# Attention, a Fourier mix and a feed-forward layer on one core: two blocks of the first layer share a PSUM bank

## The chip, the cores and the metric

The kernel runs on one core of a Trainium2 chip. The metric is device time in microseconds (us): the median over several executions. Before the change it is 1330.21 us, from 3 runs between 1328.94 and 1335.06.

A core has five engines that work at the same time, each through a queue of its own in order: TensorE (PE; its weight loads are listed as PEld), VectorE (DVE), ScalarE (ACT), GpSimd (POOL) and SyncE (SP, which here only issues transfers). PE writes its results into PSUM, a memory of eight banks, each with 512 fp32 values per partition. ACT and DVE read them from there.

## What is computed

```python
def reference(q, k, v, w_ch1, w_ch2):      # q, k, v: (8, 8, 576, 64)
    x = block_causal_attention(q, k, v)    # softmax, blocks of 64; laid out (8, 576, 512)
    X = fft(fft(x, axis=1), axis=2)
    u = x + real(X)
    un = (u - mean(u)) / sqrt(var(u) + 1e-6)          # over the last axis
    return u + maximum(un @ w_ch1, 0) @ w_ch2         # 512 -> 2048 -> 512
```

## The kernel before

**Three kinds of work.** For each of 64 heads: maxima of the scores (`max_part`, line 371), scores and exponentials (`scores`, line 417) and the product with V (`values`, line 441). For each of 8 batches: the Fourier mix (`fourier_steps`, line 522), by matmuls with cosine and sine tables. And the feed-forward: the 4,608 rows are cut into 18 feeds of 256 rows (`feed_steps`, line 725), each of which starts when its rows are normalized and turned (`normalized_steps`, line 678).

**Precision.** Products are made from fp16 parts: a value is split into a high and a low part, and three matmuls (high x high, low x high, high x low) stand for one. So an intermediate has to leave PSUM twice: as its rounded high part, and as the difference to it.

**A feed.** The hidden layer of 2,048 is cut into 16 blocks of 128. The first layer of block f is the function `first` (line 729): four parts of three matmuls, each with 256 moving columns, into one half (256 of 512 columns) of a bank of the pool `h`, which has two banks. Behind the fourth part ACT writes `gh`, the relu in fp16 (line 743), and DVE writes `gl`, what is left of it (line 744). `gh` and `gl` have three buffers each. The second layer of block f is `second` (line 746): for each half of the rows three matmuls of 512 columns (with `gh` twice and with `gl` once) are added into one of two banks `acc`. After block 15 DVE adds the result to `u` (line 755), and SP stores it. All matmuls are issued by a helper, so that their line is 194 (line 197 for transposes). In the profile the tiles tell them apart: `h<-uh,W` and `h<-ul,W` for the first layer, `acc<-W,gh` and `acc<-W,gl` for the second.

**The order inside a feed** (lines 776 to 780): the first layer of block 0, then always the first layer of block f+1 and the second layer of block f.

**The planner.** The order in which instructions are issued is made at build time, by a loop at line 909. Work comes in steps (`Step`, line 137): a cost on PE in us, a chain of costs on other engines (A for ACT, D for DVE, G for POOL, Q for SP's queue), the keys that must be done before, and the key that it sets. The planner keeps a clock `now` for PE and a list of booked times for each other engine. It picks, among the steps of attention and the transform that are ready, the one with the earliest place. Where none is ready it takes the next step of the feeds, the filler, if that is ready. The lines that matter here:

```python
yield Step(
    lambda part=part: first(f, part), 0.327, ("A0.4", "D0.44") if last else (), after,
    ("g", me, f) if last else None,
)
```

Here 0.327 is the cost of three matmuls on PE, and A0.4 and D0.44 are what ACT and DVE are booked for at the end of a block. The key `("g", me, f)` says when block f has left PSUM: `second_steps(f)` waits for it, and `first_steps(f + 2)`, which takes the same bank. The queues of ACT and DVE follow the order in which the steps are issued, whichever kind of work they belong to.

Up to the first feed the three matmul pools (`ps`, `h`, `acc`) are lent to attention as well (`lent`, line 252). From then on attention and the transform have the three banks `ps` alone. The first feed (`me == 1`) also waits for its weights (`"w"`).

Of the kernel before, what the change touches and what calls it, by code (L numbers as in the profile page):

```python
# [9 lines left out]
F32 = mybir.dt.float32  # L10
F32R = mybir.dt.float32r
F16 = mybir.dt.float16
# [10 lines left out]
P = 128  # L23
NF = FF // P
NK = DM // P
# [153 lines left out]
def tile_attn_fourier_ffn(  # L179
# [5 lines left out]
    work = pool("work")  # L185
    ps_av = pool("ps_av", 1, space=PSUM)
    ps = {name: pool(name, n, space=PSUM) for name, n in BANKS.items()}
# [5 lines left out]
    def mm(*args, **kw):  # L193
        return tc.keep_in_program_order(nc.tensor.matmul(*args, **kw))  # L194
# [43 lines left out]
    for at in range(0, NCOS, P):  # L238
        w = min(P, NCOS - at)
        nc.vector.tensor_scalar(ZT[:, at:at + w], ones[0:34, 0:w], 0.0, None, op0=ALU.mult)  # L240

    W = const.tile([P, 2 * NF + 2, 2, DM], F16, name="W")
# [14 lines left out]
    def ready(step):  # L257
        r = max((done[x] for x in step.after), default=0.0)
        return max(r, min(rings[x][0] for x in lent)) if step.bank else r
# [418 lines left out]
    def normalized_steps(us, keys, stores, place):  # L678
# [17 lines left out]
        def turn(i):  # L696
            un = uns.pop(i)
            if i == 0:
                parts.extend(work.tile([P, NK, 2, P], F16, name=x, bufs=2) for x in ("uh", "ul"))
            uh, ul = parts  # L700
            t = ps_tile()
            for c in range(NK):
                tp(t[:, P * c:P * (c + 1)], un[:, P * c:P * (c + 1)], ident)
            tv = t.rearrange("p (c n) -> p c n", c=NK)
            nc.scalar.copy(uh[:, :, i], tv)
            nc.vector.tensor_tensor(ul[:, :, i], tv, uh[:, :, i], op=ALU.subtract)
            if i == 1:
                feeds.append(feed_steps(me, uh, ul, us, stores))
# [16 lines left out]
    def feed_steps(me, uh, ul, us, stores):  # L725
        acc = []
        gs = {}

        def first(f, part):
            fs = slice(P * (f % NK), P * (f % NK + 1))  # L730
            if part == 0:
                gs[f] = ps["h"].tile([P, 512], F32, name="h")[:, 0:2 * P]
            t = gs[f]
            i = 3 * part
            for w, x_ in ((0, uh), (0, ul), (1, uh)):
                mm(t, W[:, NK * (f // NK) + part, w, fs], x_[:, part], start=(i == 0), stop=(i == 3 * NK - 1))
                i += 1
            if part < NK - 1:
                return
            gh = work.tile([P, 2 * P], F16, name="gh", bufs=3)  # L740
            gl = work.tile([P, 2 * P], F16, name="gl", bufs=3)
            gs[f] = gh, gl
            nc.scalar.activation(gh, t, AF.Relu)  # L743
            nc.vector.scalar_tensor_tensor(gl, t, 0.0, gh, op0=ALU.max, op1=ALU.subtract)  # L744

        def second(f, n):
            if f == 0:
                acc.append(ps["acc"].tile([P, DM], F32, name="acc"))
            gh, gl = gs[f]
            ns = slice(P * n, P * (n + 1))  # L750
            for j, (g_, w) in enumerate(((gh, 0), (gh, 1), (gl, 0))):
                mm(acc[n], g_[:, ns], W[:, NF + f, w], start=(f == 0 and j == 0), stop=(f == NF - 1 and j == 2))
            if f == NF - 1:
                u = us[n]
                nc.vector.scalar_tensor_tensor(u, acc[n], inv_w, u, op0=ALU.mult, op1=ALU.add)
                stores[n](u)

        def first_steps(f):
            for part in range(NK):
                last = part == NK - 1  # L760
                after = (("t", me, 0), ("t", me, 1)) + ((("g", me, f - 2),) if f > 1 else ()) if part == 0 else ()
                if me == 1:
                    after += (("w", NK * (f // NK) + part),)
                yield Step(
                    lambda part=part: first(f, part), 0.327, ("A0.4", "D0.44") if last else (), after,
                    ("g", me, f) if last else None,
                )

        def second_steps(f):
            for n in range(2):  # L770
                yield Step(
                    lambda n=n: second(f, n), 0.648, ("D0.76",) if f == NF - 1 else (), (("g", me, f),) + ((("w", NF + f),) if me == 1 else ()),
                    ("F", me) if f == NF - 1 and n == 1 else None,
                )

        yield from first_steps(0)
        for f in range(NF):
            if f + 1 < NF:
                yield from first_steps(f + 1)
            yield from second_steps(f)  # L780


    stage = [utile() for _ in range(3)]
# [125 lines left out]
    while True:  # L909
# [22 lines left out]
        if soon:  # L932
            i = min(soon, key=lambda i: heads[i].place)
        elif feed and ready(filler) <= now or feed and not able:
            i = None
        elif able:
            i = min(able, key=lambda i: ready(heads[i]))
# [60 lines left out]
```

## Time and profile before

| | |
|---|---|
| median of 3 runs | 1330.21 us |
| profiled execution, its own time | 1334.54 us |
| its span, first to last instruction | 1332.8 us |
| PE busy | 1193.2 us, 90% |
| DVE, ACT, POOL busy | 53%, 43%, 40% |
| mean granted clock of PE | 0.963 of full speed |
| matmuls of the feeds, first to last | from 186 us to the end |

An engine is busy while one of its instructions runs. A wait is the idle time before an instruction, and it is put down to whatever released that instruction last. A duration in a timeline reaches from an instruction's start to its acknowledged end; the next instruction of the engine can start before that. Idle time of an engine that is not the bottleneck costs nothing by itself.

### The profile page before, as it was taken

The page shows a single profiled execution, that of the slowest core. Times are in us where ns is not written, and L with a number is a line of the kernel's source. Part 1 is how long each engine was busy: PE and PEld are TensorE (multiplying, and loading weights), DVE is VectorE, ACT ScalarE, POOL GpSimd, SP SyncE. Part 2 cuts the span into 40 slices and gives each one's busy share as a digit, 9 for nine tenths or more (in the row PEclk, how much of TensorE's full clock was granted, in tenths as well). Part 3 has the DMA queues.
Part 4 walks back from the last instruction along what each step waited for, and adds up shares of the span by engine and source line. Part 5 has one row for each costly group of instructions (what it writes and reads, how often), then busy time and mean ns, then how long its engine had stood idle before and what let it go on. Part 6 is the DMA issues. An engine that isn't in the chain of part 4 may idle for free.

```text
span 1332.8 us, 25628 instructions
## 1 busy us (share of the span) xinstructions
PE 1193.2 (90%) x10068; PEld 892.8 (67%) x10068; DVE 702.9 (53%) x1584; ACT 567.2 (43%) x1281; POOL 533.1 (40%) x578
## 2 busy tenths in 40 slices
PE   2565379999999998999999998999999999999998
PEld 2455257767776776767777676777767667666665
DVE  6984687565646757564555654457433433312221
ACT  3569357544545555445545444454322212111111
POOL 4479244546544853654544474344600302100000
PEclk9997679989899999999999898999999999999999
DMA  9655313332332233234333223230011000000000
GB/s 281 218 154 176 108 32 83 99 91 60 82 103 76 61 85 105 59 80 108 94 80 96 65 60 90 75 96 25 21 32 34 23 17 21 17 1 17 16 17 16
DMA packets 55943, 99.10 MB, mean 74 GB/s; under 512 B 7709, under 2 KB 26605, under 8 KB 55696
## 3 DMA queue, kind: packets, MB, share of 16 engines
q1 hardware_dynamic: 52176, 87.56, 23.4%
q0 software_dynamic: 2288, 7.54, 1.9%
q10 hardware_dynamic: 1360, 2.38, 0.6%
q8 instruction: 79, 1.29, 0.4%
q14 instruction: 40, 0.33, 0.1%
HBM read 58.46 MB, written 18.87 MB: 58 GB/s over the span
## 4 chain that ended last, share of the span: by engine, by line
PE 71%; DVE 9%; POOL 4%; ACT 3%; issue 2%; DMA 2%; DVEq 0%; SPq 0%; POOLq 0%; ACTq 0%
PE h L194 25%; PE acc L194 25%; PE ps L194 14%; PE av L194 5%; POOL pl L436 2%; DVE tmp L549 2%; PE ps L197 1%; DVE M L392 1%; DMA U<-xd,rows 1%; DVE rest L308 1%; DVE tmp L550 1%; DVE fs L518 1%; DVE W L856 1%; DVE gl L744 1%; ACT lead L293 1%
## 5 line engine op out<-in xcount | busy, mean ns | idle before, releaser
L194 PE MATMUL h<-uh,W 128*128 128x256 f16 x2304 | 455.3, 276 | 0.0
L436 POOL TENSOR_TENSOR pl<-p,ph 128x288 f16<-128x288 f32 (+1 forms) x256 | 256.8, 1013 | 355.6 <-ACT p L435 229.6
L194 PEld LDWEIGHTS <-W 128*128 128x128 f16 x3456 | 325.4, 99 | 89.9 <-issue 5.4
L194 PE MATMUL acc<-W,gh 128*128 128x512 f16 x1152 | 348.6, 385 | 0.0
L194 PE MATMUL h<-ul,W 128*128 128x256 f16 x1152 | 316.7, 275 | 0.0
L744 DVE SCALAR_TENSOR_TENSOR gl<-h,gh 128x256 f16<-128x256 f32 x288 | 120.8, 420 | 294.2 <-ACT gh L743 292.5
L743 ACT ACTIVATE gh<-h 128x256 f16<-128x256 f32 x288 | 110.2, 383 | 369.1 <-PE h L194 358.6
L194 PE MATMUL acc<-W,gl 128*128 128x512 f16 x576 | 220.8, 383 | 5.3 <-DVE gl L744 5.2
L194 PE MATMUL ps<-lead 72*128 72x64 f32 (+9 forms) x696 | 198.4, 344 | 9.7 <-ACT lead L293 6.7
L434 ACT ACTIVATE ph<-ps 128x288 f16<-128x288 f32 (+1 forms) x236 | 119.7, 508 | 94.2 <-PE ps L194 92.8
L194 PE MATMUL av<-VH,pl 128*128 128x65 f16 x960 | 118.6, 202 | 38.8 <-POOL pl L436 36.9
L194 PEld LDWEIGHTS <-gh 128*128 128x128 f16 x1152 | 101.8, 99 | 65.6 <-issue 6.8
L392 DVE TENSOR_REDUCE M<-ps 128x1 f32<-128x320 f32 (+3 forms) x227 | 117.3, 531 | 43.1 <-PE ps L194 41.9
L194 PEld LDWEIGHTS <-ph 128*128 128x128 f16 x1920 | 114.6, 104 | 36.4 <-issue 12.3
L194 PEld LDWEIGHTS ps<-lead 73*128 73x128 f32 (+1 forms) x696 | 125.7, 200 | 19.0 <-ACT lead L293 6.7
L194 PE MATMUL av<-VH,ph 128*128 128x65 f16 x960 | 120.8, 203 | 14.7 <-DVE x L474 11.8
L194 PE MATMUL ps<-rest 128*128 128x64 f32 (+2 forms) x357 | 126.3, 360 | 4.0 <-DVE M L392 3.3
L310 POOL TENSOR_TENSOR rest<-raw,lead 64x576 fp32r<-64x576 f32 x64 | 117.8, 1840 | 24.7 <-ACT lead L293 19.3
L435 ACT ACTIVATE p<-ps 128x288 f32<-128x288 f32 (+1 forms) x236 | 119.5, 507 | 13.0 <-POOL pl L436 10.2
L194 PEld LDWEIGHTS <-pl 128*128 128x128 f16 x960 | 94.7, 103 | 42.4 <-POOL pl L436 40.3
L194 PE MATMUL av<-VL,ph 128*128 128x64 f16 x960 | 120.0, 201 | 0.0
L194 PEld LDWEIGHTS <-gl 128*128 128x128 f16 x576 | 56.8, 99 | 77.8 <-DVE gl L744 9.5
(171 smaller groups left out, 1393.7 us busy)
## 6 DMA issues: line engine op xcount, KB each, us to landing
raw<-in_qk_dram SPq DMA_DIRECT2D x64, 288.0 KB
rest<-lead SPq DMA_DIRECT2D x112, 144.0 KB
W<-in_moe_w_ch_dram SPq DMA_DIRECT2D x14, 1024.0 KB
V<-in_v_dram SPq DMA_DIRECT2D x32, 320.0 KB
xd<-x SPq DMA_DIRECT2D x32, 256.0 KB
out_dram<-u SPq DMA_DIRECT2D x32, 256.0 KB
u<-xd SPq DMA_DIRECT2D x8, 512.0 KB
dft<-in_c_dft_dram POOLq DMA_DIRECT2D x1, 2606.0 KB
```

The source lines that it names most:

```text
L194: return tc.keep_in_program_order(nc.tensor.matmul(*args, **kw))
L197: return tc.keep_in_program_order(nc.tensor.transpose(*args, **kw))
L293: nc.scalar.copy(LEAD[h % NB][0:D, 64:], raws[h])
L308: nc.vector.tensor_tensor(x0[0:D, 0:S], raw[:, 0:S], x1[0:D, 64:64 + S], op=ALU.subtract)
L310: nc.gpsimd.tensor_tensor(x0[D:P, S:], raw[:, S:], x1[0:D, 64 + S:], op=ALU.subtract)
L392: nc.vector.tensor_reduce(m[:, j:j + 1], t[:, at - hi:at], axis=AX.X, op=ALU.max)
L434: nc.scalar.activation(ph[:, at:at + w], t[:, 0:w], AF.Exp, scale=0.125)
L435: nc.scalar.activation(p32[:, 0:w], t[:, 0:w], AF.Exp, scale=0.125)
L436: nc.gpsimd.tensor_tensor(pl[:, at:at + w], p32[:, 0:w], ph[:, at:at + w], op=ALU.subtract)
L549: nc.vector.tensor_tensor(e[0:r], X[c][0:r], U[c][0:r], op=op)
L743: nc.scalar.activation(gh, t, AF.Relu)
L744: nc.vector.scalar_tensor_tensor(gl, t, 0.0, gh, op0=ALU.max, op1=ALU.subtract)
```

## The change

Blocks are handled in pairs. The even block takes the left half of a bank of `h`, the odd block the right half. Only the first matmul of the even block clears the bank (`start`), and only the last of the odd block closes it (`stop`). Then one ACT instruction and one DVE instruction, of 512 columns each, take both blocks out; `gh` and `gl` are twice as wide and have two buffers each in place of three. The order inside a feed goes by pairs: the first layers of blocks 0 and 1, then always the first layers of the next pair and the second layers of the pair before. The planner's steps follow: the chain (now A0.6, D0.72) hangs on the last part of the odd block, the key `("g", me, f)` stands for a pair, and the first layer of an even block waits for the pair two before. The number of matmuls and their shapes stay.

```diff
@@ feed_steps
         def first(f, part):
             fs = slice(P * (f % NK), P * (f % NK + 1))
-            if part == 0:
-                gs[f] = ps["h"].tile([P, 512], F32, name="h")[:, 0:2 * P]
-            t = gs[f]
+            if f % 2 == 0 and part == 0:
+                gs[f] = ps["h"].tile([P, 512], F32, name="h")
+            t = gs[f - f % 2]
+            half = t[:, 2 * P * (f % 2):2 * P * (f % 2 + 1)]
             i = 3 * part
             for w, x_ in ((0, uh), (0, ul), (1, uh)):
-                mm(t, W[:, NK * (f // NK) + part, w, fs], x_[:, part], start=(i == 0), stop=(i == 3 * NK - 1))
+                mm(
+                    half, W[:, NK * (f // NK) + part, w, fs], x_[:, part], start=(f % 2 == 0 and i == 0),
+                    stop=(f % 2 == 1 and i == 3 * NK - 1), skip_group_check=True,
+                )
                 i += 1
-            if part < NK - 1:
+            if f % 2 == 0 or part < NK - 1:
                 return
-            gh = work.tile([P, 2 * P], F16, name="gh", bufs=3)
-            gl = work.tile([P, 2 * P], F16, name="gl", bufs=3)
-            gs[f] = gh, gl
+            gh = work.tile([P, 4 * P], F16, name="gh", bufs=2)
+            gl = work.tile([P, 4 * P], F16, name="gl", bufs=2)
+            for x in range(2):
+                gs[f - 1 + x] = (gh[:, 2 * P * x:2 * P * (x + 1)], gl[:, 2 * P * x:2 * P * (x + 1)])
             nc.scalar.activation(gh, t, AF.Relu)
             nc.vector.scalar_tensor_tensor(gl, t, 0.0, gh, op0=ALU.max, op1=ALU.subtract)
...
         def first_steps(f):
             for part in range(NK):
-                last = part == NK - 1
-                after = (("t", me, 0), ("t", me, 1)) + ((("g", me, f - 2),) if f > 1 else ()) if part == 0 else ()
+                last = f % 2 == 1 and part == NK - 1
+                after = ()
+                if part == 0 and f % 2 == 0:
+                    after = (("t", me, 0), ("t", me, 1)) + ((("g", me, f - 4),) if f > 3 else ())
                 if me == 1:
                     after += (("w", NK * (f // NK) + part),)
                 yield Step(
-                    lambda part=part: first(f, part), 0.327, ("A0.4", "D0.44") if last else (), after,
-                    ("g", me, f) if last else None,
+                    lambda part=part: first(f, part), 0.327, ("A0.6", "D0.72") if last else (), after,
+                    ("g", me, f - 1) if last else None,
                 )
...
-                    lambda n=n: second(f, n), 0.648, ("D0.76",) if f == NF - 1 else (), (("g", me, f),) + ((("w", NF + f),) if me == 1 else ()),
+                    lambda n=n: second(f, n), 0.648, ("D0.76",) if f == NF - 1 else (),
+                    (("g", me, f - f % 2),) + ((("w", NF + f),) if me == 1 else ()),
...
         yield from first_steps(0)
-        for f in range(NF):
-            if f + 1 < NF:
-                yield from first_steps(f + 1)
-            yield from second_steps(f)
+        yield from first_steps(1)
+        for f in range(0, NF, 2):
+            for steps in (first_steps, second_steps):
+                for x in range(2):
+                    if steps is second_steps:
+                        yield from steps(f + x)
+                    elif f + 2 < NF:
+                        yield from steps(f + 2 + x)
```

## Rows read from the trace of the kernel before

**Rows 1.** The page, part 1: busy time, share of the span, instructions

```profile
PE 1193.2 (90%) x10068; PEld 892.8 (67%) x10068; DVE 702.9 (53%) x1584; ACT 567.2 (43%) x1281; POOL 533.1 (40%) x578
```

**Rows 2.** Busy time by stage: window, its length, busy (instructions) per engine, clock, DMA

```profile
0.00:186.00 186.00, 91.20 (x688) 77.48 (x689) 137.75 (x257) 99.92 (x200) 103.29 (x103) 0.86 0.55 172
186.00:966.00 780.00, 741.95 (x6882) 567.31 (x6883) 454.35 (x1082) 399.41 (x909) 396.08 (x420) 0.97 0.29 77
966.00:1332.80 366.80, 360.08 (x2501) 248.03 (x2499) 110.79 (x247) 67.90 (x173) 33.77 (x55) 1.00 0.06 19
```

**Rows 3.** Waits of PE in 186 to 966: total, times, longest

```profile
PE av L194 <- POOL pl L436: 12.9, 11, 4.2
PE ps L194 <- DVE M L392: 7.2, 7, 2.7
...
PE acc L194 <- DVE gl L744: 3.1, 3, 1.7
```

**Rows 4.** Waits of PE from 966 to the end

```profile
PE acc L194 <- DVE gl L744: 2.1, 2, 1.8
```

**Rows 5.** Timeline 1151 to 1154, a steady stretch: start, length, instruction, [idle before]

```profile
1151.14 0.38 ACT L743 ACTIVATE gh<-h 128x256 f16<-128x256 f32 x1 [2.22 <-PE h L194]
...
1151.56 0.42 DVE L744 SCALAR_TENSOR_TENSOR gl<-h,gh 128x256 f16<-128x256 f32 x1 [2.18 <-ACT gh L743]
...
1153.54 0.59 PE L194 MATMUL acc<-W,gh 128*128 128x512 f16 x2
```

**Rows 6.** Timeline 971 to 977, the longest late eviction

```profile
971.80 0.38 ACT L743 ACTIVATE gh<-h 128x256 f16<-128x256 f32 x1 [2.22 <-PE h L194]
...
976.14 0.42 DVE L744 SCALAR_TENSOR_TENSOR gl<-h,gh 128x256 f16<-128x256 f32 x1
...
976.62 0.39 PE L194 MATMUL acc<-W,gl 128*128 128x512 f16 x1 [1.82 <-DVE gl L744]
```

**Rows 7.** Timeline, PE's three other waits for gl, and waits soon after

```profile
214.91 0.39 PE L194 MATMUL acc<-W,gl 128*128 128x512 f16 x1 [0.67 <-DVE gl L744]
...
742.50 0.39 PE L194 MATMUL acc<-W,gl 128*128 128x512 f16 x1 [1.71 <-DVE gl L744]
...
745.22 0.24 PE L194 MATMUL av<-VH,ph 128*128 128x65 f16 x1 [1.15 <-DVE M L394]
...
907.12 0.39 PE L194 MATMUL acc<-W,gl 128*128 128x512 f16 x1 [0.74 <-DVE gl L744]
...
910.45 1.09 PE L194 MATMUL ps<-dft,fs 128*128 128x290 f32 x3 [1.27 <-DVE fs L518]
```

**Rows 8.** Groups of 186 to 966, shapes apart: busy us, mean ns, idle before

```profile
L744 DVE SCALAR_TENSOR_TENSOR gl<-h,gh 128x256 f16<-128x256 f32 x160 | 66.7, 417 | 73.3 <-ACT gh L743 71.5 <-issue 1.2
L434 ACT ACTIVATE ph<-ps 128x512 f16<-128x512 f32 x110 | 66.0, 600 | 33.2 <-PE ps L194 32.1
...
L743 ACT ACTIVATE gh<-h 128x256 f16<-128x256 f32 x160 | 61.1, 382 | 126.3 <-PE h L194 115.8 <-DVE vacc L333 5.0 <-PE ps L194 3.4
...
L706 DVE TENSOR_TENSOR ul<-ps,uh 128x512 f16<-128x512 f32 x20 | 13.4, 679 | 1.4 <-ACT uh L705 1.4
```

**Rows 9.** Timeline of ACT, three in a row without a wait

```profile
806.58 0.59 ACT L435 ACTIVATE p<-ps 128x512 f32<-128x512 f32 x1
807.06 0.39 ACT L743 ACTIVATE gh<-h 128x256 f16<-128x256 f32 x1
807.32 0.62 ACT L434 ACTIVATE ph<-ps 128x512 f16<-128x512 f32 x1
```

**Rows 10.** Windows at the lower clock, behind late evictions

```profile
742.90:749.70 6.80, 5.65 (x35) 4.48 (x34) 2.79 (x9) 0.40 (x1) 0.00 (x0) 0.50 0.00 1
...
910.10:913.50 3.40, 3.05 (x10) 2.26 (x11) 3.34 (x10) 1.33 (x3) 0.00 (x0) 0.50 0.00 0
```

**Rows 11.** Two of eight equal windows of 186 to 966

```profile
478.50:576.00 97.50, 92.74 (x870) 70.54 (x869) 60.43 (x147) 48.81 (x112) 50.98 (x57) 1.00 0.33 85
...
771.00:868.50 97.50, 91.80 (x809) 68.74 (x810) 47.22 (x120) 44.82 (x101) 51.09 (x60) 0.95 0.27 73
```

## The prediction

> **What bounds the kernel now.** I read the page's list of engines first: TensorE (PE) is busy for 90% of the span, and no other engine is above 53% [rows 1]. That share is an average over three stages, so the second view is the busy time by stage [rows 2]. Up to 186 us PE has no feed-forward work yet and is idle for 94.8 us; the diff leaves this stage alone, since no block of the first layer runs in it. From 186 to 966 attention, the transform and the feed-forward share the engines; PE is busy for 741.95 of 780 us, so it is idle for 38.05. From 966 on, only the rest of the transform and the feed-forward are left, and PE is idle for 366.8 - 360.08 = 6.7 us, most of it behind its last matmul, where the result leaves. PE is the bound, and the feed-forward is what fills it wherever attention leaves room: whatever is not done by 966 is done after it. So the time moves by two things only: PE's own work, and PE's idle time or slower clock.
>
> The third view is who PE waits for. In the middle stage its largest waits are for POOL's `pl` (12.9 us) and for DVE's maxima (7.2 us), both in the attention heads; the feed-forward's own wait, for `gl`, is 3.1 us in three pieces [rows 3]. In the last stage the waits for `gl` are PE's only ones: 2.1 us in two pieces [rows 4]. These 5.2 us are all that PE loses directly to the eviction that the change rewrites. The timeline of a steady stretch shows why it is so little: a block's relu starts at 1151.14, `gl` is finished at 1151.56 + 0.42 = 1151.98, and the second layer first reads that block at 1153.54 [rows 5]. There are 1.56 us to spare, since the second layer of the block before and the first layer of the block behind stand between.
>
> **The change, part by part.**
>
> *PE's work.* The 12 matmuls of a block and the 6 of its second layer stay, with the same shapes and weights; only their order and two flags differ. Cost nothing: the engine that bounds issues the same list.
>
> *The evictions.* Out go 2 ACT instructions of 0.382 us and 2 DVE instructions of 0.417 us for each pair of blocks; in come one of each over 512 columns. The trace has no relu of that width, but it has ACT reading 128x512 from PSUM into f16 in 0.600 us and DVE subtracting into 128x512 f16 in 0.679 us [rows 8]; I take these. By durations a pair saves 2 x 0.382 - 0.600 = 0.164 us on ACT and 2 x 0.417 - 0.679 = 0.155 on DVE; over the 80 pairs of the middle stage (160 blocks, [rows 8]) that is 13 and 12 us. But durations overlap when instructions stand in a row: there the 512-wide one holds ACT for 807.06 - 806.58 = 0.48 us and the relu of 256 columns for 807.32 - 807.06 = 0.26 [rows 9], so a pair frees only 2 x 0.26 - 0.48 = 0.04 us, 3 us in the stage. The freed share is 1 to 3% of what ACT (399.41 us) and DVE (454.35 us) do there [rows 2]. PE's waits there other than for `gl` are 38.05 - 3.1 = 35 us; if they shrink by as much, that is 0.3 to 1.1 us. Bounds: nothing, and 13 us if every microsecond freed on ACT were one that PE waits for. I take **-0.5**, near the low end, because the largest of these waits is for POOL, which gets nothing.
>
> *The order.* Before, a block's second layer follows its last first-layer matmul by one second-layer and one first-layer block, about 2.4 us from the relu's start [rows 5]; afterwards by two of each, about twice that. The pair's eviction takes 0.600 + 0.679 = 1.28 us, so 1.56 us to spare become 2 x 2.4 - 1.28 = 3.5, or 2 more. At the head of a feed one block stands between before, two afterwards. In the last stage DVE finished one `gl` at 976.56, although its relu began at 971.80, because DVE's queue had transform work ahead of it; PE lost 1.82 us [rows 6]. The 2 us more to spare cover that, and the other 0.3 us of that stage [rows 4]. Nothing follows there that would wait for DVE instead, since all that PE still does is feed-forward: **-2.1**.
>
> In the middle stage it is otherwise. Two of the three waits fell while DVE was far behind, and PE met DVE again soon after: 1.15 us at 745.22, behind the wait at 742.50, and 1.27 us at 910.45, behind the one at 907.12 [rows 7]. PE takes its instructions in order; arriving earlier, it would wait there for as much longer. Of 3.1 us only the 0.67 at 214.91 has no wait for DVE close behind it: **-0.7**, with ends 0 and -3.1.
>
> *Buffers.* The two banks and two pairs of `gh`/`gl` hold as many blocks as the order needs: pair k takes the bank of pair k-2, and its `gh` buffer, after all of pair k-1's first layer and pair k-2's second have been issued. Cost nothing in steady order; the cover is that distance, and if it is gone the price is the eviction of 1.28 us itself. No DMA is added, and no queue of SP or POOL is passed.
>
> *The planner.* The order of PE is written by a planner with new costs and due times, so from the first feed on attention's steps fall elsewhere among the blocks, and the 35 us of other waits and the slower stretches are dealt anew. I count this as nothing on average. For its size I use how the eight equal windows of the stage differ. In the one that loses least PE is idle for 97.5 - 92.74 = 4.8 us at full clock; in the one that loses most it is idle for 5.7, and a clock of 0.95 takes another 4.9 [rows 11], together 10.6. So a window deals some 2 us either way of the middle of these, and eight of them, if independent, 2 x the root of 8, about 6 us: an estimate.
>
> **Sum:** -0.5 - 2.1 - 0.7 = -3.3 us. The rows are of an execution that took 1334.54 us (a span of 1332.8 and 1.7 around it), 4.3 above the median of 1330.21; I take the difference from the median: **1327 us**, and 0.25% is not to be told from nothing (a measurement of this kernel tells about 0.5%, 6.65 us, from no change).
>
> **The rivals.**
>
> *A, faster: the waits for `gl` also cost clock.* Behind the wait at 742.50 the granted clock is 0.50 (the 1.2 GHz level) for 6.8 us, and behind that at 907.12 for 3.4 us [rows 10], with PE busy almost throughout, so half of each is lost. If the late evictions go and nothing takes their place, the gain is 5.2 + 3.4 + 1.7 + 0.5 = 10.8: 1319.4 us. For it: in both stretches PE had just been idle. Against it: the waits behind them [rows 7] would leave PE idle as well.
>
> *B, slower: the longer instruction stands in front of a head.* A pair's relu holds ACT 0.218 us longer than a block's, and its `gl` DVE 0.262 longer, in one piece. Where they come just ahead of the exponentials that `pl` is made from, or of a maximum, PE's 11 + 7 waits for these [rows 3] each grow by 0.48: 8.6 us, 1338.8 us. It decides from 14 of those 18 (6.65 / 0.48) on. For it: both queues are in order. Against it: there are half as many such pieces, and POOL, not ACT, is the late one in 11 of the 18.
>
> *C, much slower: the banks no longer rotate.* The first block of a pair now waits in its bank until the second is done, and its eviction no longer lies beside the second's matmuls; if PE had to stand by, all 144 pairs would pay 1.28 us, 184 us: 1514 us. Against it: two banks are left, and 4.8 us between a pair and its reader. The Trainium skill, Perfetto Trace Analysis, "Optimizing Tensor Performance", asks that independent groups of matmuls rotate through different PSUM banks so that one's evacuation overlaps the next one's matmuls; inside a pair the change does the opposite. The trace bears it out so far as [rows 5] have the eviction beside the next block's matmuls; but that block's partner can stand there as well as the next pair.
>
> **How the numbers follow.** The forecast (no measurable change) has a chance of 0.51, A 0.33, B 0.14, C 0.02. So faster by over 0.5% is 0.33, within it 0.51, slower 0.16. The range starts below A, at 1314, where A meets a part of the 13 us bound on the freed time, and ends at 1337, between the planner's 6 us and a little more over the forecast and B. The forecast's own range is 1319 to 1335.
>
> **What would show it.** ACT's and DVE's groups on `h` should have 144 instructions each, near 0.60 and 0.68 us. PE's matmuls should be as many and as long. PE's waits for `gl` should be under 1 us in all, and PE after 966 idle only at the end. Waits for `pl` and the maxima should stay near 20 us. The prediction is wrong if PE's idle time between 186 and 966 falls or rises by more than 6 us, if the lower clock shows clearly less or more often, or if the 512-wide evictions take much more than the rows say.

## The result: 1317 us, and the profile after

The changed kernel takes 1317.41 us (median of 9 runs, 1312.82 to 1322.97) against 1330.44 for the kernel before (9 runs, 1326.45 to 1335.06). The ratio is 0.9904, 95% interval 0.9887 to 0.9921: about 13 us faster, and clear of the 0.5% bound. That is inside the range given (1314 to 1337), on the side that had a chance of 0.33, and just below the forecast's own range (1319 to 1335).

The profiled execution took 1312.82 us, the fastest of the nine; its span is 21.9 us shorter than that of [rows 1], while the medians differ by 13.0. The two profiles therefore show in sum more gain than there is.

The groups of the two evictions, with the columns of [rows 8], but over the whole span (from the page):

```profile
L750 DVE SCALAR_TENSOR_TENSOR gl<-h,gh 128x512 f16<-128x512 f32 x144 | 98.8, 686 | 232.4 <-ACT gh L749 232.0
...
L749 ACT ACTIVATE gh<-h 128x512 f16<-128x512 f32 x144 | 85.9, 597 | 292.4 <-PE h L194 292.2
```

Half as many (144 pairs in 288 blocks), at 0.597 and 0.686 us; 0.600 and 0.679 were assumed.

A steady stretch of the last stage, to be read against [rows 5]:

```profile
1154.07 0.60 ACT L749 ACTIVATE gh<-h 128x512 f16<-128x512 f32 x1 [4.61 <-PE h L194]
...
1154.70 0.69 DVE L750 SCALAR_TENSOR_TENSOR gl<-h,gh 128x512 f16<-128x512 f32 x1 [4.52 <-ACT gh L749]
...
1159.08 0.59 PE L194 MATMUL acc<-W,gh 128*128 128x512 f16 x2
```

The reader starts 1159.08 - 1154.07 = 5.0 us behind the relu's start, and the pair is out at 1155.39: 3.7 us to spare, where there were 1.56. PE has no wait for `gl` left in the whole span, and no wait of any kind after 966 us. Its waits in the middle stage, against [rows 3]:

```profile
PE av L194 <- POOL pl L436: 10.4, 10, 2.7
PE ps L194 <- DVE M L392: 8.1, 10, 2.0
```

The busy times by stage, against [rows 2] (same columns):

```profile
186.00:966.00 780.00, 749.64 (x6919) 574.16 (x6917) 451.75 (x1001) 389.53 (x820) 389.08 (x414) 0.98 0.29 77
966.00:1310.90 344.90, 340.83 (x2454) 236.97 (x2453) 94.61 (x175) 57.78 (x115) 38.81 (x61) 1.00 0.06 19
```

PE's idle time in the middle stage fell from 38.05 to 30.4 us, that of the last from 6.7 to 4.1. The clock records of the two traces have 47.8 and 25.7 us at the lower level (0.50, 1.2 GHz) inside the middle stage; at half speed that is up to 23.9 and 12.9 us of full-speed work lost (PE is busy in 44.5 and 20.4 us of that time). The differences are 7.7 + 2.6 + 11.0 = 21.3 us, where the spans differ by 21.9. Only 5.2 us of idle time were waits for `gl`. The rest of the gain is somewhere that the sum had counted as nothing, and the experiments ask where.

### The profile page after: what moved, and what is told of

Read it like the earlier page. It is cut to its first block, busy times and chain, and to the rows that moved or that the text cites. A ratio compares the mean times of both kernels' runs of the same rounds, so it can differ in the third digit from the quotient of the medians.

```text
span 1310.9 us, 25271 instructions
## 1 busy us (share of the span) xinstructions
PE 1181.7 (90%) x10068; PEld 888.4 (68%) x10068; DVE 684.6 (52%) x1440; ACT 548.8 (42%) x1137; POOL 532.6 (41%) x578
## 3 DMA queue, kind: packets, MB, share of 16 engines
q1 hardware_dynamic: 52176, 87.56, 23.6%
## 4 chain that ended last, share of the span: by engine, by line
PE 73%; DVE 10%; DMA 3%; POOL 3%; issue 2%; ACT 1%; SPq 0%; DVEq 0%; POOLq 0%; ACTq 0%
PE acc L194 26%; PE h L194 25%; PE ps L194 15%; PE av L194 5%; PE ps L197 2%; DVE tmp L549 1%; DVE M L392 1%; POOL pl L436 1%; DVE tmp L550 1%; DMA lead<-mt 1%; DVE rest L308 1%; DMA xd<-x 1%; DMA U<-xd,rows 1%; POOL u L538 1%; DMA u<-in_moe_w_ch_dram 1%
## 5 line engine op out<-in xcount | busy, mean ns | idle before, releaser
L194 PE MATMUL h<-uh,W 128*128 128x256 f16 x2304 | 433.5, 275 | 0.0
L436 POOL TENSOR_TENSOR pl<-p,ph 128x288 f16<-128x288 f32 (+1 forms) x256 | 260.6, 1029 | 368.0 <-ACT p L435 186.6
L194 PE MATMUL acc<-W,gh 128*128 128x512 f16 x1152 | 344.2, 380 | 0.0
L750 DVE SCALAR_TENSOR_TENSOR gl<-h,gh 128x512 f16<-128x512 f32 x144 | 98.8, 686 | 232.4 <-ACT gh L749 232.0
L749 ACT ACTIVATE gh<-h 128x512 f16<-128x512 f32 x144 | 85.9, 597 | 292.4 <-PE h L194 292.2
L194 PEld LDWEIGHTS ps<-lead 72*128 72x128 f32 (+1 forms) x696 | 126.7, 200 | 22.0 <-ACT lead L293 7.7
L310 POOL TENSOR_TENSOR rest<-raw,lead 64x576 fp32r<-64x576 f32 x64 | 116.9, 1826 | 25.9 <-ACT lead L293 20.4
L308 DVE TENSOR_TENSOR rest<-raw,lead 64x576 fp32r<-64x576 f32 x64 | 65.2, 1019 | 94.5 <-ACT lead L293 92.5
```

The costliest lines, as they stand in the source:

```text
L308: nc.vector.tensor_tensor(x0[0:D, 0:S], raw[:, 0:S], x1[0:D, 64:64 + S], op=ALU.subtract)
L310: nc.gpsimd.tensor_tensor(x0[D:P, S:], raw[:, S:], x1[0:D, 64 + S:], op=ALU.subtract)
L436: nc.gpsimd.tensor_tensor(pl[:, at:at + w], p32[:, 0:w], ph[:, at:at + w], op=ALU.subtract)
```

## Experiments

All were timed in five rounds beside the kernel before, in three sets (e1 to e4, e5 to e8, e9 to e12; its medians there are 1330.8, 1331.8 and 1330.0 us). Ratios are to that kernel, with 95% intervals; they are the recorded ones, and differ from the quotient of the two medians by up to 0.0014. Three theories stand against each other. *Relief*: the merged instructions free ACT and DVE. *Blocks* (or *order*): the blocks' own order, with the reader a pair away. *Deal*: the planner, run with other costs and due times, puts attention's matmuls elsewhere among the feeds (an order of the whole work is called a deal here), and this order happens to be better.

### 1. Same order, evictions split again (e1_split_evictions)

```diff
-            nc.scalar.activation(gh, t, AF.Relu)
-            nc.vector.scalar_tensor_tensor(gl, t, 0.0, gh, op0=ALU.max, op1=ALU.subtract)
+            for x in range(2):
+                s = slice(2 * P * x, 2 * P * (x + 1))
+                nc.scalar.activation(gh[:, s], t[:, s], AF.Relu)
+                nc.vector.scalar_tensor_tensor(gl[:, s], t[:, s], 0.0, gh[:, s], op0=ALU.max, op1=ALU.subtract)
```

> The changed kernel with its order, its planner costs and its buffers, but each pair leaves the bank in two ACT and two DVE instructions of 256 columns. Theory 'order' (the gain comes from where the blocks stand in PE's order: the reader is a whole pair away): as fast as the changed kernel, ratio to before 0.988 to 0.993, no waits of PE for gl after 966. Theory 'relief' (the gain comes from the ACT and DVE time that the merged instructions free): the gain is gone, ratio 0.997 to 1.003.

Measured: 1319.99 us, ratio 0.9921 (0.9898 to 0.9944). With four instructions for a pair in place of two, most of the gain is there, and PE never waits for `gl`. PE's order is that of the changed kernel, so the distance to 0.9904 is the price of the splitting: 2 us as measured, and by the two intervals anything from nothing to 6 us. The groups show what was put back:

```profile
L752 DVE SCALAR_TENSOR_TENSOR gl<-h,gh 128x256 f16<-128x256 f32 x288 | 120.6, 419 | 245.9 <-ACT gh L751 245.0
...
L751 ACT ACTIVATE gh<-h 128x256 f16<-128x256 f32 x288 | 110.0, 383 | 337.1 <-PE h L194 256.3 <-DVE gl L752 80.1
```

24 us of busy time on ACT and 22 on DVE are back in the whole span (110.0 - 85.9, 120.6 - 98.8), and little of it reaches the end. *Relief* is the smaller part at most, and may be nothing.

### 2. Merged evictions, short distance (e2_interleaved)

```diff
-        for f in range(0, NF, 2):
-            for steps in (first_steps, second_steps):
-                for x in range(2):
-                    if steps is second_steps:
-                        yield from steps(f + x)
-                    elif f + 2 < NF:
-                        yield from steps(f + 2 + x)
+        for f in range(NF):
+            if f + 2 < NF:
+                yield from first_steps(f + 2)
+            yield from second_steps(f)
```

> The changed kernel with merged evictions, but the first layer of a block and the second layer of a block take turns again (first layer of f+2, then second layer of f), so that only one block stands between a pair's last matmul and its reader. Theory 'order': the gain is lost or turned round, PE waits for gl several times as often as before (over 10 us in all), ratio 1.00 to 1.02. Theory 'relief': as many instructions as in the changed kernel, ratio 0.988 to 0.994.

Measured: 1324.65 us, ratio 0.9954 (0.9936 to 0.9972). Neither expectation: half the gain went, yet PE waited for `gl` once, for 0.9 us, not for 10. The planner takes a feed's step only when it holds it for ready, and otherwise issues attention's steps, so a shorter distance need not show as waits: it shows as another order. A change to the feeds' steps is thus always a change of the whole deal as well; this run can't separate the two.

### 3. Only the planner's figures (e3_booked_as_two, e4_before_booked_less)

On the changed kernel (e3), and on the kernel before (e4):

```diff
-                    lambda part=part: first(f, part), 0.327, ("A0.6", "D0.72") if last else (), after,
+                    lambda part=part: first(f, part), 0.327, ("A0.8", "D0.88") if last else (), after,
...
-                    lambda part=part: first(f, part), 0.327, ("A0.4", "D0.44") if last else (), after,
+                    lambda part=part: first(f, part), 0.327, ("A0.3", "D0.36") if last else (), after,
```

> The changed kernel, but the planner books a pair's eviction at the price of two single ones (A0.8, D0.88). The instructions of a pair stay as they are; the planner deals another order. Theory 'order' and theory 'relief': the gain stays within some 6 us, ratio 0.985 to 0.995. Theory 'deal' (the new figures only dealt a lucky order): the gain is gone, ratio about 1.00.

> The kernel before, but the planner books each single eviction at half the price of a pair's (A0.3, D0.36). Theory 'deal' or a planner that gains by lower bookings: ratio 0.985 to 0.995. Theory 'order' and theory 'relief': no gain, ratio 0.995 to 1.005; the spread to 1.00 shows how much another deal is worth.

Measured: e3 1328.93 us, ratio 0.9989 (0.9970 to 1.0007); e4 1320.65 us, ratio 0.9932 (0.9909 to 0.9956). The changed kernel's own instructions, under another booking, give the gain away; the kernel before, its instructions untouched, gains 9 us of the 13. Both are what *deal* expects; *relief* and *blocks* expected the opposite of each.

### 4. The deal held fixed, the blocks exchanged (e5_old_deal_new_blocks, e6_new_deal_old_blocks)

A block of the first layer (4 steps of 0.327 us) and one of the second (2 of 0.648) are almost equally long. So the planner can run with one kernel's steps while what is issued in the feeds' places are the other kernel's blocks.

e5, on the kernel before, with `first` of the changed kernel:

```diff
+        ORDER = [("F", f) for f in (0, 1)] + [(k, f + x + (2 if k == "F" else 0)) for f in range(0, NF, 2) for k in "FS" for x in range(2) if k == "S" or f + 2 < NF]
+        at = [0]
+
+        def go(n):
+            for _ in range(n):
+                kind, f = ORDER[at[0] // 4]
+                r = at[0] % 4
+                at[0] += 1
+                if kind == "F":
+                    first(f, r)
+                elif r % 2 == 1:
+                    second(f, r // 2)
...
-                    lambda part=part: first(f, part), 0.327, ("A0.4", "D0.44") if last else (), after,
+                    lambda: go(1), 0.327, ("A0.4", "D0.44") if last else (), after,
...
-                    lambda n=n: second(f, n), 0.648, ("D0.76",) if f == NF - 1 else (), (("g", me, f),) + ((("w", NF + f),) if me == 1 else ()),
+                    lambda: go(2), 0.648, ("D0.76",) if f == NF - 1 else (), (("g", me, f),) + ((("w", NF + f),) if me == 1 else ()),
```

e6 is the mirror image on the changed kernel. It keeps the changed kernel's first feed, and two wide buffers each for `gh` and `gl` in place of three narrow ones. In both, the traces have the matmuls outside the feeds in the same order as in the kernel whose deal is used; the number of feed matmuls ahead of any of them differs by 0, 3 or 6.

> The planner runs with the steps and costs of the kernel before, so every matmul of attention and the transform keeps its place in PE's order (within three matmuls of the feeds); but what is issued in the feeds' places are blocks in the changed kernel's order, by pairs, with its merged evictions. Theory 'blocks' (pairs and merged evictions gain by themselves): ratio 0.988 to 0.994. Theory 'deal' (the gain came from where the planner's new figures put attention's steps): only the waits for gl go, 3 to 5 us, ratio 0.996 to 1.000.

> The other way round: the planner runs with the changed kernel's steps and costs, so attention's matmuls keep the places that they have there; but from the second feed on the blocks in the feeds' places come in the order of the kernel before, one by one, each with its own two evictions (two buffers for gh and gl; the first feed as in the changed kernel). Theory 'blocks': the gain is gone, ratio 0.997 to 1.003. Theory 'deal': most of it stays, ratio 0.990 to 0.995, with waits for gl of a few us back.

Measured: e5 1327.21 us, ratio 0.9961 (0.9945 to 0.9977); e6 1325.31 us, ratio 0.9950 (0.9931 to 0.9969). Both lie at the edge of what *deal* expected, and outside what *blocks* expected. The 13 us come apart into nearly equal halves:

| | deal before | deal after |
|---|---|---|
| **blocks before** | 1 | 0.9950 (e6) |
| **blocks after** | 0.9961 (e5) | 0.9904 |

On this deal the blocks alone gain 0.4% (5 us), the deal alone 0.5% (7 us), and together they make nearly the whole. In e5, PE's waits for `gl` are gone, and by stage it has:

```profile
186.00:966.00 780.00, 740.39 (x6915) 569.83 (x6914) 452.14 (x1006) 393.09 (x832) 398.52 (x420) 0.98 0.29 78
966.00:1326.50 360.50, 356.20 (x2471) 245.67 (x2469) 99.48 (x178) 56.20 (x107) 33.35 (x55) 1.00 0.06 18
```

In the last stage idle time fell from 6.7 to 4.3 us, as forecast (-2.1). In the middle stage it did not fall: 39.6 us against 38.05. Timeline of PE in e5, where the kernel before had its waits at 742.50 and 745.22 [rows 7]:

```profile
745.69 0.20 PE L194 MATMUL av<-VH,ph 128*128 128x65 f16 x1 [3.97 <-DVE M L394]
```

PE no longer stops for `gl`, comes to the next instruction that needs DVE earlier, and stands there for 3.97 us, where it stood for 1.15 before. The late engine was still late: a wait removed in front of it was a wait moved. In part it is so at the other place, too. The kernel before waits 0.74 us for `gl` at 907.12 [rows 7], and then for ACT:

```profile
908.78 0.40 PE L194 MATMUL ps<-dft,fs 128*128 128x290 f32 x1 [0.86 <-ACT fs L517]
```

e5 has no wait for `gl` there, and the one for ACT is longer:

```profile
905.46 0.40 PE L194 MATMUL ps<-dft,fs 128*128 128x290 f32 x1 [1.44 <-ACT fs L517]
```

That the time fell by 4.6 us all the same, with only 2.4 - 1.6 = 0.8 us less idle time in the profile, goes with the clock: the lower level covers 34.1 us of that stage in this one execution, 47.8 in that of the kernel before, or up to 6.9 us of work. Little of that lies where the waits for `gl` were: near 742 the lower level shrank from 6.8 to 3.4 us, near 907 it stayed at 3.4. Whether the blocks cause the rest, or the executions merely differ, one profile of each can't say.

e6 has the waits for `gl` back:

```profile
PE acc L194 <- DVE gl L768: 3.9, 6, 1.0
```

### 5. Other deals (e7 to e10)

One constant of the planner that has nothing to do with the blocks, on either kernel (by how much a step of attention must have been ready, on the planner's clock, to go ahead of a ready step of the feeds):

```diff
-MARGIN = 0.3
+MARGIN = 0.25
```

(0.35 in e9 and e10.)

> The kernel before with one constant of the planner changed that has nothing to do with the blocks (MARGIN 0.25 in place of 0.3), to see what another deal is worth. If deals differ by chance: somewhere in 0.990 to 1.008. If the kernel before sits at a typical deal: 0.997 to 1.003.

> The changed kernel with the same constant changed (MARGIN 0.25). If the gain belongs to the blocks or to lower bookings as such, it stays: 0.987 to 0.994. If it was one lucky deal: about 0.997 or above.

> The kernel before with the same constant of the planner moved to the other side (MARGIN 0.35). Theory 'the deal before is a poor one of many': 0.988 to 0.998, most likely near 0.993. Theory 'the deal before is typical and the one at 0.25 a lucky one': 0.997 to 1.005.

> The changed kernel with MARGIN 0.35. If the blocks gain 0.4% whatever the deal, and the deal is drawn anew: 0.984 to 0.999, on average below the kernels with single blocks by 0.004. If the changed kernel is at a typical deal of its own: 0.988 to 0.993.

Measured: e7 1317.07 us, ratio 0.9894 (0.9871 to 0.9918); e8 1319.26, 0.9911 (0.9889 to 0.9934); e9 1321.33, 0.9926 (0.9901 to 0.9950); e10 1338.15, 1.0071 (1.0046 to 1.0095). The kernel before, with one unrelated number changed, is as fast as the changed kernel; the changed kernel, with the same number moved the other way, is slower than the kernel before. e8 alone came where a gain that belongs to the blocks or to lower bookings was expected; e7 (by less than its interval) and e10 lie outside every range given for them, and e9 where it was expected if the deal before is a poor one of many. PE by stage in e7 and then in e10:

```profile
186.00:966.00 780.00, 747.10 (x6996) 574.00 (x6995) 452.66 (x1103) 403.12 (x919) 397.37 (x423) 0.98 0.29 78
966.00:1314.00 348.00, 343.44 (x2381) 236.47 (x2379) 99.45 (x223) 62.84 (x161) 31.09 (x52) 1.00 0.05 17
```

```profile
186.00:966.00 780.00, 742.73 (x6806) 568.46 (x6805) 455.35 (x980) 382.47 (x805) 385.56 (x409) 0.98 0.28 77
966.00:1330.30 364.30, 356.12 (x2567) 247.93 (x2565) 104.38 (x199) 65.35 (x131) 43.52 (x65) 0.99 0.06 19
```

In e7 PE is idle for 32.9 us in the middle stage, in e10 for 37.3, and for 8.2 in the last. e10 waits nowhere for `gl`; it waits for the heads' maxima:

```profile
PE ps L194 <- DVE M L392: 11.0, 12, 2.3
PE av L194 <- POOL pl L436: 8.9, 11, 2.5
PE ps L197 <- DVE M L394: 4.1, 4, 2.0
```

### 6. New blocks on two other deals (e11, e12)

e5's edit on the deals of e7 and of e4.

> As the kernel with the old deal and the new blocks, but with the deal of MARGIN 0.25, which had 0.9894 with the old blocks. If the blocks gain some 4 to 5 us whatever the deal: 0.984 to 0.988, faster than the changed kernel. If they gain only where the deal is poor: 0.988 to 0.991.

> The same with the deal of the kernel before booked at A0.3 and D0.36, which had 0.9932 with the old blocks. If the blocks gain some 4 to 5 us whatever the deal: 0.988 to 0.991. If they gain only where the deal is poor: 0.992 to 0.994.

Measured: e11 1316.71 us, ratio 0.9886 (0.9861 to 0.9910), against 0.9894 for e7; e12 1321.32, 0.9924 (0.9898 to 0.9951), against 0.9932 for e4. Both are 0.0008 below the old blocks on the same deal, 1 us, and not told from nothing; by the quotients of the medians both are 0.0011 above. Each of these two differences has an interval of 0.0035 either way, so neither alone rules out a gain of 5 us; but both ratios missed the range for one that comes whatever the deal. The blocks measured 0.0039 and 0.0046 on one pair of deals and 0.0008 on the other pair. e11 is the fastest kernel measured, but its interval overlaps with that of the changed kernel, so no version that beats both is shown.

### The ledger

From the profiled execution of each kernel: PE's idle time in two stages, the time at the lower clock in the middle one, and what is left of the span when idle time and half of the lower-clock time are taken off. (e10 has 8.8 us more at the lower clock after 966, e3 3.4, the others up to 2.2. The first feed starts between 184.0 and 187.6 us, in before at 186.2, in after at 184.2; that is in the last column, too.)

| kernel | span | idle 186-966 | lower clock 186-966 | idle from 966 | left |
|---|---|---|---|---|---|
| before | 1332.8 | 38.0 | 47.8 | 6.7 | 1264 |
| after | 1310.9 | 30.4 | 25.7 | 4.1 | 1264 |
| e1 | 1314.8 | 29.8 | 29.9 | 4.1 | 1266 |
| e2 | 1319.1 | 35.0 | 30.7 | 4.3 | 1264 |
| e3 | 1327.2 | 32.9 | 51.2 | 6.8 | 1262 |
| e4 | 1317.2 | 31.9 | 27.3 | 6.1 | 1266 |
| e5 | 1326.6 | 39.6 | 34.1 | 4.3 | 1266 |
| e6 | 1319.7 | 30.4 | 39.3 | 5.3 | 1264 |
| e7 | 1314.0 | 32.9 | 29.8 | 4.6 | 1262 |
| e8 | 1317.4 | 29.3 | 41.0 | 5.5 | 1262 |
| e9 | 1315.1 | 32.2 | 29.9 | 5.4 | 1263 |
| e10 | 1330.4 | 37.3 | 36.5 | 8.2 | 1267 |
| e11 | 1316.3 | 33.3 | 30.7 | 4.1 | 1264 |
| e12 | 1322.3 | 33.0 | 37.5 | 4.3 | 1266 |

The last column moves little (1262 to 1267), while the span moves by 22 us. The three columns between are nearly the whole story of these kernels: when PE stands still among attention's work, and how long its clock stays low there.

The table also shows what the deal sets. Kernels that share a deal share the idle time of the middle stage to within 1.6 us, whatever their blocks: 38.0 and 39.6 us (before, e5), 30.4, 30.4 and 29.8 (after, e6, e1), 32.9 and 33.3 (e7, e11), 31.9 and 33.0 (e4, e12). The idle time of the last stage is 4.1 to 4.3 in these kernels with the new blocks, and 4.6 to 6.7 with the old. The lower clock goes by neither: 47.8 and 34.1, 25.7, 39.3 and 29.9, 29.8 and 30.7, 27.3 and 37.5, one execution of each. So with the deal held fixed, the idle time of both stages together fell by only 0.1 to 1.2 us through the new blocks.

## Why the prediction was right or wrong

**PE as the bound, and idle time and clock as the only ways the time can move:** right in the main; in the ledger they leave 5 us between the kernels, where the spans differ by 22.

**The evictions (-0.5).** Sizes right (0.597 and 0.686 us for 0.600 and 0.679). That the freed time is worth little was right: giving it back cost 2 us, not told from nothing (e1).

**The order, last stage (-2.1).** Right: no wait left there, idle time from 6.7 to 4.3 in e5 and 4.1 after; 3.7 us to spare for the 3.5 worked out.

**The order, middle stage (-0.7).** The mechanism was right, and more so than was counted: with the deal held fixed, the waits for `gl` went and the idle time did not (39.6 us for 38.05, where -0.7 was forecast), since PE met DVE again and waited there (3.97 us at 745.69).

**The planner (counted as nothing on average, some 6 us either way).** This is the step that failed. With the old blocks the new deal alone measured 0.9950, 6.7 us, more than all terms of the sum together. The size was there as an estimate, the place in its spread was not: the kernel before had the slowest of the five deals tried with its blocks (1, 0.9950, 0.9932, 0.9926, 0.9894). What that term held is idle time: on the new deal the middle stage has 30.4 us of it with either blocks, on the old one 38.0 and 39.6. That the deal before was a slow one, no single trace shows. The estimate from the eight windows was also too small for the new steps: their four deals are 0.9904, 0.9911, 0.9989 and 1.0071, a spread of 22 us.

**Rival A** named a time (1319.4) near the measured one, for another reason: it wanted the late evictions gone with nothing in their place, and something did take their place. Of the 5.1 us of its clock term the trace of e5 has 1.7: half of the 3.4 us less near 742, and nothing near 907. **Rival B** (a longer piece in front of the heads) is not refuted by the 18.5 us of waits for `pl` and the maxima after against 20.1 before, since the deal differs. With the deal held fixed they went from 20.1 to 23.6 (e5), 17.8 to 18.5 (e6 to after), 11.6 to 11.5 (e7 to e11) and 11.2 to 12.5 (e4 to e12): at most 3.5 of its 8.6 us, and whether that is the longer piece or waits that moved is not shown. **Rival C** (banks that no longer rotate) did not show: no wait for an eviction of `h` was left.

**The sum.** The blocks alone, on the deal before, measured about 5 us against 3.3 worked out. That these are close is in part luck: the sum counted idle time, and of that only 0.8 us went in e5; the rest goes with the clock, at which the sum put nothing. The changed kernel came out 10 us below the forecast, 7 of them the deal. That 1317 is still inside the range is luck as well: its lower end came from rival A and from the time freed on ACT and DVE, and neither made the gain. Of the prediction's own signs of being wrong two came true: the idle time of the middle stage fell by 7.7 us, where 6 was the bound, and the lower clock shows for 25.7 us in place of 47.8.

What stays open: why the blocks are worth 0.4% on two deals and 0.1% on two others. The last stage's waits for `gl` explain some (2.1 us on the deal before), not all. In the profiles the lower clock of the middle stage goes the same way: 13.7 and 13.6 us less with the new blocks on the first two deals, 0.9 and 10.2 us more on the others. Why it does, and whether it would in other executions, is not shown.

## What to carry to other kernels

Where a program writes the order of the work, any edit to a step's cost or due time deals the whole order anew. Before such an edit is credited with a gain, change a constant that should not matter: here that alone moved the same kernel by 14 us (e7), as much as the edit did. To learn what an edit itself is worth, hold the order fixed and exchange only what stands in its places.

And a wait on an engine that is behind need not be saved by reading its result later, if PE soon after needs the same engine again, as at 742 here.

## What the runs showed of the hardware that was not expected

The lower clock before the first feed costs little here: e1 has 89.5 us at the lower level up to 186 us and the kernel before 51.2, with 94.8 us of idle PE time in both, and the first `h<-uh,W` starts at 187.58 and 186.19 us, 1.4 us apart where half of the difference in clock would be 19. For that reason the mean granted clock of an execution says little: of the nine of the changed kernel, one of 1322.97 us has 0.968 and one of 1316.68 has 0.958. After 186 us it counts, as in the ledger. The longest stretch there at the lower level in the changed kernel follows four waits of PE between 331 and 338 us, 2.6 us in all:

```profile
338.00:358.50 20.50, 15.26 (x103) 12.66 (x103) 11.26 (x27) 9.08 (x19) 15.36 (x21) 0.50 0.24 63
```

PE is busy for 15.26 of these 20.5 us, at half speed.
